# Leaving SyncE out of a skipped fallback: a two-way switch on four engines in place of an If on all five, with the fallback's DMAs issued by GpSimd

## Chip, cores, metric

One core of a Trainium2 chip. The metric is the device time of an execution in microseconds (us), given as the median of several executions. A profile is one such execution; its "span", the time from its first to its last instruction, is shorter than its measured time by 1.8 us here (before: 780.63 against 778.8).

## The reference

```python
def reference(A_x, A_wq, A_wk, A_wv, A_wo, B_x, B_w_gate, B_w_up, B_w_down):
    # A: attention, H = 32 query heads of 16, one shared key/value head; x is 1 x 2048 x 512, bf16
    #    q = x@wq; k = x@wk; v = x@wv; p = softmax(q k^T * 16**-0.5); o = p v; return o @ wo
    # B: (silu(x @ w_gate) * (x @ w_up)) @ w_down, with 1792 hidden columns
    x = A_x
    xn = _layernorm(x, axis=-1)
    s = _A_ref(xn, A_wq, A_wk, A_wv, A_wo)
    g = _silu(_B_ref(xn, B_w_gate, B_w_up, B_w_down))
    return x + s * g
```

## The kernel before

The kernel computes the softmax without subtracting row maxima. At the end it checks whether every denominator lies between 16 and 1e30. If one doesn't, a flag is set and a long exact path computes everything anew. With the inputs the flag is 0 and the exact path is jumped over. What matters here is the end of the program: the flag, the last four row blocks, their stores, and the conditional.

```python
    # flag: 1 if any of the 128 partition minima says "out of range"
    tadd("DVE", e_out_mul(LN, obk[0], dsts[0]))
    tadd("DVE", nc.vector.tensor_single_scalar(out=flag_i[:], in_=tq01[0:1, 0:1], scalar=P - 0.5, op=ALU.is_lt))
    loads, vals = nc.values_load_multi_w_load_instructions(flag_i[0:1, 0:1])   # all five engines
    flag = vals[0]
    tadd("SP", [l for l in loads if l.ins.engine == nc.sync.engine])
    fin_add(0, nc.gpsimd, "POOL")
    tadd("DVE", e_out_mul(LN + 1, obk[1], dsts[1]))
    tadd("DVE", e_out_mul(LN + 2, obk[2], dsts[2]))
    fin_add(2, nc.gpsimd, "POOL")
    tadd("DVE", [l for l in loads if l.ins.engine == nc.vector.engine])
    fin_add(1, nc.vector, "DVE")
    tadd("DVE", e_out_mul(LN + 3, obk[3], dsts[3]))
    fin_add(3, nc.vector, "DVE")
    for k in range(4):
        tadd("SP", e_out_st(LN + k))          # the last four stores, 128 KB each, on SyncE's queue
    MAIN.close()

    with tc.If(flag > 0):
        _exact_max_path(...)                  # long; its DMAs are nc.sync.dma_start
```

`tadd` fixes the order on an engine. In `_exact_max_path` three lines start DMAs (cut):

```python
                        nc.sync.dma_start(out=MR[row:row + 1, :], in_=tms[r0:r0 + NT, :])
    # ...
            nc.sync.dma_start(out=xr[:], in_=x_v[:, n, :])
    # ...
            nc.sync.dma_start(out=out_v[:, n, :], in_=res[:])
```

## Time and profile before

| | before |
|---|---|
| time, median of 3 | 781.96 us (780.98 to 782.83) |
| span of the profiled execution | 778.8 us |
| flag made, start | 769.94 us |
| VectorE's last add ends | 773.44 us |
| last store: issued, landed | 773.81, 776.07 us |
| SyncE's gap after its branch | 774.2 to 776.9 us |
| from the flag to the end of the span | 8.9 us |

"Landed" is the time of the last of a store's 16 semaphore updates; each is taken to stand for the part that one of the 16 DMA engines moves (the trace doesn't name the engine).

### The profile page before, as it was taken

The page shows a single profiled execution, that of the slowest core. Times are in us where ns is not written, and L with a number is a line of the kernel's source. Part 1 is how long each engine was busy: PE and PEld are TensorE (multiplying, and loading weights), DVE is VectorE, ACT ScalarE, POOL GpSimd, SP SyncE. Part 2 cuts the span into 40 slices and gives each one's busy share as a digit, 9 for nine tenths or more (in the row PEclk, how much of TensorE's full clock was granted, in tenths as well). Part 3 has the DMA queues.
Part 4 walks back from the last instruction along what each step waited for, and adds up shares of the span by engine and source line. Part 5 has one row for each costly group of instructions (what it writes and reads, how often), then busy time and mean ns, then how long its engine had stood idle before and what let it go on. Part 6 is the DMA issues. An engine that isn't in the chain of part 4 may idle for free.

```text
span 778.8 us, 20698 instructions
## 1 busy us (share of the span) xinstructions
PE 748.9 (96%) x9093; PEld 229.7 (29%) x9095; DVE 734.0 (94%) x920; ACT 756.9 (97%) x866; POOL 54.2 (7%) x59
## 2 busy tenths in 40 slices
PE   8999999999999999999999999999999999999995
PEld 3323223322222333322233322322223233322221
DVE  7689999999999999999999999999999999999995
ACT  6999999999999999999999999999999999999993
POOL 2100000000012000000001110000000300000101
PEclk9999999999999999999999999999999999999998
DMA  9400000000001000000000100000000000000001
GB/s 327 141 9 9 16 2 24 3 8 17 4 28 50 23 2 6 18 2 24 2 10 22 49 24 2 24 1 9 16 2 24 28 23 2 2 23 3 22 2 32
DMA packets 21193, 20.15 MB, mean 26 GB/s; under 512 B 8744, under 2 KB 17192, under 8 KB 21096
## 3 DMA queue, kind: packets, MB, share of 16 engines
q1 hardware_dynamic: 19512, 18.20, 7.7%
q8 instruction: 73, 1.20, 0.6%
q10 hardware_dynamic: 1584, 0.56, 0.3%
q14 instruction: 24, 0.20, 0.1%
HBM read 14.19 MB, written 2.34 MB: 21 GB/s over the span
## 4 chain that ended last, share of the span: by engine, by line
PE 48%; ACT 45%; DVE 5%; issue 1%; SPq 0%; DMA 0%; ACTq 0%; POOL 0%; DVEq 0%; POOLq 0%
ACT Pb L937 41%; PE ring L877 17%; PE m_ps L488 16%; PE o_ps L747 13%; ACT th L657 3%; DVE Bf L997 1%; ACT g_sb L937 1%; PE ring L433 1%; DVE Bf L1016 1%; ACT th L674 1%; DVE x_sb L997 0%; DVE Bf L1023 0%; PE ring L488 0%; DVE x_sb L1016 0%; PE ring L452 0%
## 5 line engine op out<-in xcount | busy, mean ns | idle before, releaser
L937 ACT ACTIVATE Pb<-ring 128x1024 bf16<-128x1024 f32 x772 | 730.7, 1202 | 2.1 <-PE ring L877 2.1
L877 PE MATMUL ring<-QB,KT 32*128 32x512 bf16 x2048 | 306.0, 382 | 15.6 <-ACT Pb L937 9.3
L997 DVE TENSOR_SCALAR Bf<-ring 128x1024 uint16<-128x1024 f32 x172 | 209.2, 1216 | 5.2 <-PE ring L877 3.7
L877 PEld LDWEIGHTS <-KT 32*128 32x128 bf16 x2048 | 94.1, 90 | 313.9 <-issue 307.4
L747 PE MATMUL o_ps<-Pb,VA 128*32 128x512 bf16 x1544 | 146.9, 385 | 0.0
L997 DVE TENSOR_SCALAR x_sb<-ring 128x1024 uint16<-128x1024 f32 x72 | 87.6, 1217 | 2.7 <-PE ring L877 2.4
L1016 DVE TENSOR_TENSOR Bf<-Bf,Bf 128x2048 f16<-128x2048 f16 x74 | 90.0, 1216 | 0.1
L747 PE MATMUL o_ps<-xnT,zw 128*32 128x512 bf16 x1092 | 83.1, 381 | 0.0
L488 PE MATMUL m_ps<-xnT,wu_sb 128*32 128x512 bf16 x896 | 72.6, 384 | 1.1 <-DVE ab L659 1.1
L488 PE MATMUL m_ps<-wd_sb,hT 128*32 128x512 bf16 x896 | 71.5, 383 | 0.1
L488 PE MATMUL m_ps<-xnT,wg_sb 128*32 128x512 bf16 x896 | 70.4, 384 | 0.0
L747 PE MATMUL o_ps<-Bf,VD 128*32 128x512 f16 x688 | 67.1, 385 | 0.4 <-DVE Bf L1016 0.3
L732 POOL TENSOR_TENSOR oT<-oa,rb 128x512 bf16<-128x512 f32 x15 | 22.7, 1514 | 614.2 <-DMA rb<-dscr 515.7
L1023 DVE TENSOR_SCALAR Bf<-Bf 128x2048 uint16<-128x2048 uint16 x86 | 60.4, 702 | 0.6
L747 PEld LDWEIGHTS <-VA 128*32 128x32 bf16 x1560 | 38.0, 94 | 53.8 <-issue 51.5
L1011 DVE TENSOR_SCALAR Bf<-Bf 128x2048 uint16<-128x2048 uint16 x74 | 52.1, 712 | 0.0
L657 ACT ACTIVATE th<-m_ps 128x512 f32<-128x512 f32 x56 | 43.7, 781 | 0.0
L659 DVE SCALAR_TENSOR_TENSOR ab<-th,m_ps 128x512 f32<-128x512 f32 x56 | 38.1, 680 | 4.2 <-ACT th L657 3.9
L663 DVE TENSOR_TENSOR hT<-ab,m_ps 128x512 bf16<-128x512 f32 x56 | 38.1, 680 | 2.1 <-PE m_ps L488 1.7
L747 PEld LDWEIGHTS <-VD 128*32 128x32 f16 x976 | 26.6, 94 | 38.9 <-issue 35.3
L747 PEld LDWEIGHTS <-zw 128*32 128x32 bf16 x1092 | 25.8, 95 | 25.5 <-issue 12.9
L1016 DVE TENSOR_TENSOR x_sb<-x_sb 128x2048 f16<-128x2048 f16 x24 | 29.2, 1215 | 0.0
(121 smaller groups left out, 414.3 us busy)
## 6 DMA issues: line engine op xcount, KB each, us to landing
rb<-dscr SPq DMA_DIRECT2D x15, 256.0 KB
out_dram<-xn SPq DMA_DIRECT2D x16, 128.0 KB, 1.9
dn<-oa SPq DMA_DIRECT2D x120, 2.0 KB, 1.7
oa<-oa SPq DMA_DIRECT2D x60, 32.0 KB, 2.0
wg_sb<-in_B_w_gate_dram SPq DMA_DIRECT2D x1, 1792.0 KB, 12.3
wu_sb<-in_B_w_up_dram SPq DMA_DIRECT2D x1, 1792.0 KB
wd_sb<-in_B_w_down_dram SPq DMA_DIRECT2D x1, 1792.0 KB, 19.7
x_sb<-in_A_x_dram SPq DMA_DIRECT2D x3, 512.0 KB
```

Of the source, the lines that this page charges most:

```text
L488: return [nc.tensor.matmul(out=dst[GRP * j:GRP * j + GRP, :], lhsT=w[:, GRP * j:GRP * j + GRP], rhs=rhs, start=start, stop=stop, tile_posi ...
L657: t_ = OP("ACT", 0.477, [a], lambda: nc.scalar.activation(out=th[i][:], in_=m_ps[:], func=ACT.Tanh, scale=0.5), (0,), name="tanh")
L659: s_ = OP("DVE", 0.6, [t_, ab_rel[i]], lambda: nc.vector.scalar_tensor_tensor(out=ab[i][:], in0=th[i][:], scalar=1.0, in1=m_ps[:], op0=ALU ...
L663: h = OP("DVE", 0.6, [b], lambda: nc.vector.tensor_tensor(out=hT[:, f, :], in0=ab[i][:], in1=m_ps[:], op=ALU.mult), (1,), name="hmul")
L732: return [pk, q], lambda eng: eng.tensor_tensor(out=oT[qs % 2][:, jj, :], in0=o0[:], in1=rbt[:], op=ALU.mult)
L747: r.append(nc.tensor.matmul(out=o_ps[GRP * g:GRP * g + GRP, :], lhsT=lhs, rhs=rhs, start=(n == 0), stop=(n == pv_total[(b, g)] - 1), tile_ ...
L877: return lambda: [nc.tensor.matmul(out=ring[sl][:, u * 512:(u + 1) * 512], lhsT=KT[half][GRP * g:GRP * g + GRP, t * P:(t + 1) * P], rhs=QB ...
L937: bi = nc.scalar.activation(out=buf, in_=ring[i][:], func=ACT.Exp, scale=escale, bias=ebias)
L997: lambda: nc.vector.tensor_scalar(out=U[:, hs], in0=ring[si][:], scalar1=ubias, scalar2=UINF, op0=ALU.add, op1=ALU.min), (1.5, u), name="p ...
L1011: o1 = OP("DVE", 0.6, [pa, pa0] + wrel, lambda: nc.vector.tensor_scalar(out=Bf[wi], in0=U, scalar1=0x3FF, scalar2=0x3800, op0=ALU.bitwise_and,
L1016: return lambda: eng.tensor_tensor(out=Bf[wi][:, a:z].bitcast(FP16), in0=Bf[wi][:, a:z].bitcast(FP16), in1=U[:, a:z].bitcast(FP16), op=ALU ...
L1023: o2 = OP("DVE", 0.6, o3, lambda: nc.vector.tensor_scalar(out=U, in0=U, scalar1=0x7C00, scalar2=None, op0=ALU.bitwise_and), (2, u, 1), nam ...
```

## The change

The intent is to take SyncE out of the conditional. SyncE issues the last stores, so it comes to the branch last, and its long jump ends the program. As SyncE must then issue nothing within the fallback, the fallback's DMAs go to GpSimd, and the If becomes a two-way switch on the four other engines, whose arm 0 is empty.

```diff
@@ three lines of _exact_max_path @@
-                        nc.sync.dma_start(out=MR[row:row + 1, :], in_=tms[r0:r0 + NT, :])
+                        nc.gpsimd.dma_start(out=MR[row:row + 1, :], in_=tms[r0:r0 + NT, :])
-            nc.sync.dma_start(out=xr[:], in_=x_v[:, n, :])
+            nc.gpsimd.dma_start(out=xr[:], in_=x_v[:, n, :])
-            nc.sync.dma_start(out=out_v[:, n, :], in_=res[:])
+            nc.gpsimd.dma_start(out=out_v[:, n, :], in_=res[:])
@@ the flag @@
-    loads, vals = nc.values_load_multi_w_load_instructions(flag_i[0:1, 0:1])
-    flag = vals[0]
-    tadd("SP", [l for l in loads if l.ins.engine == nc.sync.engine])
+    arm_engines = [mybir.EngineType.PE, mybir.EngineType.Activation, mybir.EngineType.DVE, mybir.EngineType.Pool]
+    loads, vals = nc.values_load_multi_w_load_instructions(flag_i[0:1, 0:1], engines=arm_engines, min_val=0, max_val=1,
+                                                           skip_runtime_bounds_check_because="is_lt writes 0 or 1")
@@ the conditional @@
-    with tc.If(flag > 0):
+    for arm in tc.Switch({e: vals[0] for e in arm_engines}, 2):
+        if arm == 0:
+            continue
         _exact_max_path(tc, nc, wo_sb, x_v, out_v, wq_sb, xnT, KT, VA, g2_sb, ident_bf, ident_f, qscale,
```

## The prediction

> **What bounds the kernel now.** I read the page first, for what limits the body, then what stands at the end of the span, because the diff touches nothing before it. The page's busy times and slices:
>
> ```profile
> span 778.8 us, 20698 instructions
> ...
> PE 748.9 (96%) x9093; PEld 229.7 (29%) x9095; DVE 734.0 (94%) x920; ACT 756.9 (97%) x866; POOL 54.2 (7%) x59
> ```
>
> ScalarE, TensorE and VectorE are all within a few per cent of the span, and the exponentials on ScalarE (772 of 1202 ns) carry it. None of this is in the fallback: the three engines run the main path and the fallback is jumped over, as the instruction count shows. So 770 us of the span are out of the change's reach and only the end is left.
>
> The chain of waits of the last stretch, in order of time, comes next:
>
> ```profile
> 769.94 0.13 DVE flag_i L1360
> 770.07 0.57 DVE ab L690
> ...
> 771.87 0.61 DVE oa L690
> 772.48 0.02 issue
> 772.50 0.93 DVE xn L695
> ```
>
> It stops at 773.43 although the span ends at 778.8: the last 5.4 us hold no compute, only sequencers. The window sums say the same (columns: stretch, its length, then busy us and count of PE, PEld, DVE, ACT, POOL, the clock, DMA share, GB/s):
>
> ```profile
> 774.20:776.90 2.70, 0.00 (x0) 0.00 (x0) 0.00 (x0) 0.00 (x0) 0.00 (x0) 0.50 0.35 110
> 776.90:778.80 1.90, 0.00 (x0) 0.00 (x0) 0.00 (x0) 0.00 (x0) 0.00 (x0) 0.50 0.01 4
> ```
>
> The timeline of SyncE and the listing of the If's own line (duration min/median/max in ns, then first and last start) give what fills them:
>
> ```profile
> 771.35 2.83 SPq L698 DMA_DIRECT2D out_dram<-xn  x4
> ```
>
> ```profile
> L1376 SPq EVENT_SEMAPHORE  x8: 17/17/17, 776.9 to 777.4; - x8
> L1376 ACTq COMPARE_BRANCH  x1: 50/50/50, 770.6 to 770.6; - x1
> L1376 PEldq COMPARE_BRANCH  x1: 3635/3635/3635, 770.7 to 770.7; - x1
> L1376 POOLq COMPARE_BRANCH  x1: 45/45/45, 771.9 to 771.9; - x1
> L1376 DVEq COMPARE_BRANCH  x1: 72/72/72, 772.5 to 772.5; - x1
> L1376 ACTq EVENT_SEMAPHORE  x1: 17/17/17, 773.5 to 773.5; - x1
> L1376 SPq COMPARE_BRANCH  x1: 45/45/45, 774.2 to 774.2; - x1
> ...
> L1376 DVEq EVENT_SEMAPHORE  x1: 21/21/21, 775.4 to 775.4; - x1
> ```
>
> And SyncE's own waits:
>
> ```profile
> SPq L1376 <- SPq L1376: 2.6, 1, 2.6
> ```
>
> The reader is to see that after its branch at 774.2 SyncE does nothing for 2.6 us, and that nobody else is named as having released it. VectorE is silent equally long after its branch (772.6 to 775.4, 2.8 us), ScalarE too (770.7 to 773.5, 2.8 us), TensorE for 3.6 us inside the branch. GpSimd, whose body of the If is empty, goes on after 0.1 us. So these are gaps of a jump over a large body, not waits for data. For four engines the gap lies beside other work. Only for SyncE, the last to branch since it branches behind the last store, is it on the path that sets the end.
>
> **What the Trainium skill says.** "Runtime: NRT & Kernel Launch", section "Instruction fetch mechanics": prefetch is sequential, and a taken branch to a target outside the window that is loaded stalls for a fetch. The trace agrees: 2.6 to 3.6 us where a body is jumped, 0.1 us where there is none. The page names no figure for the stall. "Advanced Engine Details and Errata", section "Control Flow Timing", gives compare-and-branch some 108 ns; the trace has 45 to 72 ns for the instruction itself, so the instruction isn't the cost. "DMA: Bandwidth & Descriptors", section "Anatomy of one DMA — SWDGE (gpsimd) path", has about 2.0 us fixed for a DMA, mostly the receipt of the write; the four last stores of this trace took 2.4 to 2.7 us from issue to landing, median 2.5, so the trace's figure is used.
>
> **The change part by part.** The order of the built programs shows the main path the same instruction for instruction, apart from the flag's handling. So the first 770 us: 0.
>
> (a) SyncE loses its load of the flag (0.48 us at 770.10). It stood before the first store, but that store is issued at 771.35 as GpSimd's add of 1.15 us from 770.17 ends at 771.32. Worth 0.
>
> (b) SyncE loses its branch, and with it the 2.6 us gap and the eight semaphore steps behind it, spaced 0.07 us (776.9 to 777.4). It now runs straight from the last store into the final waits. What ends these is the landing of the last store: issued at 773.81 (771.35 + 2.83 - 0.37), landing 2.3 to 2.4 us later, so at 776.1 to 776.2. In the kernel before this landing was hidden under the gap; now it takes the gap's place. The final list of waits has twelve entries instead of eight (four more steps, for the software-queue semaphores of GpSimd), but these stand first and are passed while the landing is awaited. Behind the last store's semaphore stand six more at 0.06 us, 0.4 us. Then comes the closing barrier: from SyncE's last such wait (777.9) to the end (778.8), 0.9 us. New end: 776.1 + 0.4 + 0.9 = 777.4. Gain 778.8 - 777.4 = 1.4 us.
>
> (c) The other four replace one compare-and-branch by a register set-up, a multiply-add, an indirect branch into a short arm 0, and at its end an unconditional branch over the fallback, with a prefetch hint at the arm's start. I take an estimate of 0.3 us for the additional steps (about five at 0.05 to 0.07 us, the spacing just read). The jump of 2.8 us stays. VectorE is the latest: 772.5 + 0.3, then its count step that waits for its own last add (773.4), then 2.8 us: 776.2 if the hint gains nothing, 775.6 if it starts the fetch at once. Both are before the 776.5 at which SyncE clears its list, but not by much. TensorE: 770.6 + 0.5 + 3.6 = 774.7. GpSimd, which skipped nothing before, now has the long body: flag loaded at 771.8, 0.5 us of set-up and arm, 2.8 us: 775.1. Off the path.
>
> (d) Arm 0 on GpSimd has to bring the eight semaphores of its software queues up to the count that arm 1 would leave. It does this at about 772.5, and SyncE waits for that; a like instruction takes 27 ns at the start of this trace. Off the path.
>
> (e) The 100 or so DMAs moved to GpSimd are in arm 1, which doesn't run: 0.
>
> Sum: 0 + 1.4 + 0 = 1.4 us of 782, 0.2%.
>
> **The rivals.** First, the full gap goes: 2.6 + 0.5 = 3.1 us, some 779 us. Against it stands the landing: 2.4 us after the last issue is not gone, and nothing in the change shortens it.
>
> Second, the jump turns up on another engine. If the indirect branch into arm 0 stalls too, VectorE pays twice: 772.8 + 2.8 + 0.1 + 2.8 = 778.5, against the 778.0 at which SyncE joins the barrier now; the end would be 779.3 and the time 0.5 us longer, 782.5. For it speaks that four engines show the stall at any long jump; against it that arm 0 is the next code in order and that GpSimd's short step took 0.1 us. I give it one in five. A milder form, in which the hint's fetch queues behind another, puts VectorE near 776.7 and the gain at 1.2.
>
> Third, the stores themselves shift. The second store's issue took 1.31 us (the listing of the store line has median 361 ns, maximum 1314), and this held back the third and fourth. If it is issued in 0.4, the last store leaves when VectorE's add ends at 773.43, and the landing comes 0.3 to 0.4 us earlier: gain 1.8. It falls together with a 16 KB instruction transfer in the same window (the queue of kind "instruction" moved two there), so with more such fetches from the new branches it could as well be longer, and a further 1 us would eat most of the gain.
>
> Fourth, a use of the software queue costs something outside the span at launch. The measured time exceeds the span by about 3 us already; the queue is declared in both programs, so I expect nothing.
>
> **Range and chances.** 781.96 - 1.4 = 780.6 us. The effect itself lies between -3 and +0.5; the three runs of before spread over 1.85 us, so a median of three is good to about 0.6. Together: 779.2 to 782.0 in 8 of 10. A change of 2% would need 15.6 us, three times all that happens after the last compute; so 0.98 for within 2%, 0.01 for either side, kept for something at launch that no view shows.
>
> **What would show it.** Right: SyncE has no instruction of the If's line and no flag load; its waits name the landing of the last store instead of itself, ending near 776.1; the distance from the last store's issue to the end of the span falls from 5.0 to about 3.6 us; GpSimd and VectorE show the long gap after their new branches but reach the barrier before SyncE. Wrong in step (b): the end is not tied to the landing. Wrong in step (c): VectorE's or GpSimd's last step comes behind SyncE's, with two gaps of 2.8 us. The prediction as a whole would be wrong if the body before 769 us changed its length, for which I see no reason.

## The result, and the profile after

| | before | after |
|---|---|---|
| time, median of 4 and range | 782.24 us (780.98 to 782.83) | 782.7 us (781.48 to 783.38) |
| span of the profiled execution | 778.8 us | 781.4 us |
| flag made, start | 769.94 us | 770.12 us |
| last store: issued, landed | 773.81, 776.07 us | 775.10, 780.08 us |
| from the flag to the end | 8.9 us | 11.3 us |

All outputs are right. The ratio after to before is 1.0006, with a 95% interval of 0.9988 to 1.0025. A ratio is the mean time of one kernel's runs over that of the other's of the same rounds, so it is not quite the ratio of the medians. The kernels take the same time, as the most likely of the three classes said; but 782.7 us lies 0.7 above the predicted range, and the gain of 1.4 us isn't there.

First, whether the body moved. The page of after, then its chain of waits at the end (start, duration in us, what):

```profile
span 781.4 us, 20718 instructions
...
PE 747.5 (96%) x9093; PEld 229.2 (29%) x9095; DVE 734.1 (94%) x920; ACT 757.0 (97%) x866; POOL 54.0 (7%) x59
```

```profile
770.13 0.13 DVE flag_i L1360
...
772.69 0.93 DVE xn L695
```

The work is the same, and the compute ends at 773.62 instead of 773.44. The difference of 2.6 us between the two spans therefore arises almost wholly after the last compute. SyncE's own waits (engine, line, what it waited for: us in total, times, longest), then the timeline of SyncE:

```profile
SPq L1406 <- DMA out_dram<-xn: 2.3, 2, 2.1
SPq L1406 <- PEq L1406: 0.7, 2, 0.5
```

```profile
771.53 5.43 SPq L698 DMA_DIRECT2D out_dram<-xn  x4
```

SyncE's wait for itself is gone, and a wait for the landing of the stores stands in its place. That much is as predicted. SyncE isn't quite without a branch under the switch, though:

```profile
L1406 SPq COMPARE_BRANCH  x1: 43/43/43, 777.0 to 777.0; - x1
```

Its next instruction comes 0.4 us later, which the wait for the landing covers here.

But issuing the four stores took 5.43 us, against 2.83 before. The listing of the store's line has the reason. Its columns are the duration of one issue in ns (min/median/max), then first and last start; the line below gives the landings that the view could pair (the first and the third store). Before:

```profile
L698 SPq DMA_DIRECT2D out_dram<-xn x4: 349/378/1314, 771.3 to 773.8; - x4
...
DMA to landing us min/median/max: 2.4/2.5/2.7
```

After:

```profile
L698 SPq DMA_DIRECT2D out_dram<-xn x4: 343/1101/1882, 771.5 to 775.1; - x4
...
DMA to landing us min/median/max: 4.6/4.7/4.8
```

Before, one of four issues was long (1314 ns); after, two were (1882 and 1859 ns), and the landings, counted from the start of the issue, took about twice as long. The last store's landing was 2.7 us longer than before: 1.5 us of this is its longer issue, and nearly all of the rest comes from one late part. Of the 16 parts of after's last store, 15 had landed at 778.32 and the last at 780.08; of its first store, 14 at 773.25 and the last two at 775.51 and 776.09. So behind the issue one or two parts were late, not the store as a whole. What else ran on the DMA engines in these microseconds is in the DMA view for 771 to 775 us (queue, kind: packets, MB, share of the 16 engines' time). Before:

```profile
q14 instruction: 3, 0.02, 2.6%
q8 instruction: 1, 0.02, 1.8%
```

After:

```profile
q14 instruction: 6, 0.05, 9.4%
q8 instruction: 2, 0.03, 6.6%
```

These are fetches of instructions: four before, eight after, and together 16.0% of the DMA engines' time instead of 4.4%. Each is one packet: 16 KB on q8, 8 KB on q14. Over the whole tail there are 8 before and 13 after. q8 is taken to be TensorE's: it has 74 fetches in a span, TensorE some 18,200 matmuls and weight loads, and a hint on TensorE alone later started one there. That leaves q14 to the other engines.

Last, the new branches. The listing of the conditional's line in after:

```profile
L1406 PEldq COMPARE_BRANCH  x2: 358/2678/4998, 771.2 to 771.9; - x2
L1406 DVEq COMPARE_BRANCH  x2: 60/68/75, 772.9 to 773.8; - x2
...
L1406 DVEq DRAIN  x1: 70/70/70, 778.2 to 778.2; - x1
```

There are two branches for each engine: into arm 0, and from there over the fallback. TensorE's second branch took 5.0 us (before 3.6), and VectorE was silent from 773.8 to 778.2, 4.4 us (before 2.8). Both were ready before SyncE, whose last store landed at 780.08.

Three theories were set against each other from here. **Theory 1**: the instruction fetches of the far branches share the DMA engines with the last four stores, hold up their issues and landings, and so eat what SyncE's branch had cost. **Theory 2**: GpSimd's software-queue DMAs, and the semaphores that an engine must bring up for them in arm 0, cost the time. **Theory 3**: there is nothing there but the spread from run to run, or a fixed tail.

### The profile page after: what moved, and what is told of

Read it like the earlier page. It is cut to its first block, busy times and chain, and to the rows that moved or that the text cites. A ratio compares the mean times of both kernels' runs of the same rounds, so it can differ in the third digit from the quotient of the medians.

```text
span 781.4 us, 20718 instructions
## 1 busy us (share of the span) xinstructions
PE 747.5 (96%) x9093; PEld 229.2 (29%) x9095; DVE 734.1 (94%) x920; ACT 757.0 (97%) x866; POOL 54.0 (7%) x59
## 4 chain that ended last, share of the span: by engine, by line
PE 47%; ACT 44%; DVE 6%; issue 1%; POOL 0%; SPq 0%; DMA 0%; ACTq 0%; DVEq 0%; POOLq 0%
ACT Pb L937 39%; PE ring L877 17%; PE m_ps L488 16%; PE o_ps L747 13%; ACT th L657 3%; DVE Bf L997 1%; ACT g_sb L937 1%; DVE Bf L1016 1%; ACT th L674 1%; DVE x_sb L997 0%; DVE Bf L1023 0%; PE ring L488 0%; DVE hT L663 0%; DVE Bf L1011 0%; DVE x_sb L1011 0%
```

## The experiments

In the tables, "store issues" are the durations of the four issues in ns, "landing" is from issue to the last part's landing for the last store, and "fetches" are instruction fetches in the tail. Kernels of one group were run on the same chip and share its runs of the kernel before.

### First group: the If without SyncE, no conditional, hints, and a repeat

**if_four**: the change without the switch. SyncE is out and GpSimd issues, but the plain If stays.

```diff
 # against before: the three DMAs on nc.gpsimd and the flag loaded by four engines, as in the change
-    tadd("SP", [l for l in loads if l.ins.engine == nc.sync.engine])
     with tc.If(flag > 0):      # kept
```

> The changed kernel with the plain If in place of the Switch: SyncE takes no part, the fallback's DMAs are GpSimd's, the software-queue semaphores are there. 'Tail' is from the start of the flag's instruction on VectorE to the end of the span: 8.9 us before, 11.3 after, in the profiled runs. Theory 1 (fetch traffic: the Switch makes each of four engines fetch one more block of instructions, and these transfers hold up the last stores on the DMA engines they share): the tail is 7.0 to 7.8 us, the last store lands within 2.7 us of its issue, issues take 0.4 us but for one or two of 1.3; time 0.1 to 0.25% below before. Theory 2 (the software queue of GpSimd or its semaphores cost it): tail about 11 us as in after, stores late. Theory 3 (nothing but spread from run to run; stores are held up at random): tail anywhere from 7 to 11, time equal to after.

**no_cond**: the changed kernel with the flag still computed, but with neither the loads nor the fallback (a floor, not a kernel to use).

```diff
-    loads, vals = nc.values_load_multi_w_load_instructions(...)
-    tadd("DVE", [l for l in loads if l.ins.engine == nc.vector.engine])
-    for arm in tc.Switch({e: vals[0] for e in arm_engines}, 2):
-        ...
```

> No flag, no conditional, no fallback: the floor (right for these inputs, which never take the fallback). All theories: no engine jumps far. Theory 1: next to no instruction transfers after 770 us, four issues of 0.35 to 0.4 us, the last store lands 2.0 to 2.4 us after its issue, tail 6.3 to 6.9 us counted from the time at which the flag would be made (VectorE's first product of the last group, 0.6 us earlier, is the mark); time 0.2 to 0.35% below before. Theory 3: some stores would still be issued in over 1 us or land over 4 us late.

**if_hint**: if_four with a branch prefetch hint on each of the four engines, moved ahead of the branch.

```diff
+    tc.mark_branch_hint_location("fallback", "LikelyTaken", engines=[PE, Activation, DVE, Pool])
-    with tc.If(flag > 0):
+    with tc.If(flag > 0, label="fallback"):
+    # after the build: each hint to the 63rd (PE), 6th (ACT), 22nd (DVE), 5th (POOL)
+    # instruction from the end of its engine's main block
```

> if_four, with a prefetch hint for the If's branch on each of the four engines some microseconds ahead of it, before the last stores. Theory 1: the transfers of the targets move ahead of the stores, the gap after the branches goes from 2.8 us to under 0.5, and only the sequential fetches behind the targets are left among the stores: tail 6.5 to 7.5 us, the time equal to if_four or up to 0.1% lower. Theory 2 or 3: no better than if_four. If a hint isn't held until its branch or blocks the sequential prefetch, the gap stays or an engine stalls before the branch, and the time is that of if_four or up to 3 us longer.

**after_again**: the changed kernel once more.

> The changed kernel once more. Theory 1: tail 10 to 12 us again, with two or more of the four stores issued in over 1 us and the last landing over 3.5 us after its issue; time within 0.15% of before, on the slow side. Theory 3: the tail differs by 2 us or more from the first profiled run.

| | time (n = 5) | ratio to before (95%) | store issues, ns | landing, us | fetches | flag to end, us |
|---|---|---|---|---|---|---|
| before (n = 9) | 781.64 (780.42 to 782.29) | 1 | | | | |
| if_four | 781.56 (780.05 to 781.96) | 0.9998 (0.9985 to 1.0012) | 344, 1601, 745, 353 | 3.2 | 8 | 9.0 |
| no_cond | 778.64 (778.44 to 779.26) | 0.9963 (0.9949 to 0.9976) | 344, 344, 332, 332 | 1.7 | 1, after the stores | 6.7 |
| if_hint | 779.32 (778.99 to 779.47) | 0.9971 (0.9957 to 0.9984) | 343, 375, 1514, 450 | 1.8 | 7, and 1 ahead | 7.8 |
| after_again | 781.68 (780.48 to 782.99) | 1.0001 (0.9987 to 1.0015) | 344, 343, 1203, 2461 | 5.5 | 13 | 11.1 |

The stores of no_cond, in the listing of their line:

```profile
L698 SPq DMA_DIRECT2D out_dram<-xn x4: 332/338/344, 771.9 to 774.0; - x4
...
DMA to landing us min/median/max: 1.7/1.7/1.7
```

This is the store undisturbed: 0.34 us to issue, 1.7 us to land (2.0 to 2.4 had been expected). Theory 3 had expected issues of over 1 us or landings of over 4 us here too, and there is none. "The" landing, 2.3 to 2.5 us, was already a disturbed one. The trace of before had the floor all along, in the listing of the same line over all of its 16 stores:

```profile
L698 SPq DMA_DIRECT2D out_dram<-xn x16: 332/361/1314, 232.2 to 773.8; - x16
...
DMA to landing us min/median/max: 1.7/1.9/2.7
```

no_cond also bounds the whole question: the conditional costs 3.0 us (781.64 - 778.64). And its times lie within 0.8 us, where before's lie within 1.9: part of the spread from run to run leaves with the conditional.

if_four answers whether leaving SyncE out is worth 1.4 us by itself. SyncE's waits there:

```profile
SPq L1405 <- DMA out_dram<-xn: 2.2, 2, 1.7
```

Its gap is gone and a landing stands in its place, as in after, and the time is before's within 0.1 us. The interval reaches down to 0.9985, or 1.2 us, so a small gain isn't excluded by this group, but 1.4 is. The lost gain therefore doesn't need the switch to explain it. This was also a miss for Theory 1 as it had been put: it had laid the loss to the switch's additional fetches and expected a tail of 7.0 to 7.8 us and a time 0.1 to 0.25% below before. The If's own eight fetches are enough (tail 9.0 us, landing 3.2 us).

after_again repeats the trace of after: 13 fetches, two long issues, a late landing. Yet its median is if_four's within 0.1 us, although the traces differ by 2 us in the tail. The profiled execution of after_again took 782.73 us, its second slowest of five; if_four's took 780.97, its second fastest. So the medians don't separate switch from If, and a trace is one draw out of a spread.

if_hint gained 0.29%, more than expected (at most 0.1% below if_four). TensorE's hint started its fetch early (a 16 KB fetch at 769.08, 4.3 us before VectorE's last add ends), and its branch over the fallback shrank from 3.9 us in if_four to 0.9 us. The hints on ScalarE and VectorE started none: the gaps behind their branches remained (ScalarE 770.6 to 773.2, VectorE 772.5 to 775.9). These two hints had run at 762.2 and 760.6, and GpSimd's at 689.3: a place counted in instructions says little about the time.

### Second group: repeat of before, a later switch, no software-queue DMAs, no hints

**before_again**: the kernel before once more.

> The kernel before, profiled once more. In six traces the flag is made at 769.8 to 770.5 us, so the body is the same and only the tail differs; yet the median times of before and after are equal, though the profiled tails were 8.9 and 11.1 to 11.3. Theory 1 (instruction transfers of the branching engines hold up the last stores, in before too, and by an amount that varies from run to run): the first profiled run of before was a lucky one; a second has a tail of 9.0 to 10.8 us, with the last store landing over 2.6 us after its issue, later than SyncE's own gap ends. Theory 3 (a fixed tail of 8.9 in before, and something outside the span that favours after): tail 8.7 to 9.0 again and the time still that of after.

**switch_late**: the changed kernel with the flag made behind VectorE's last add, so that the engines branch when the stores are nearly out.

```diff
-    tadd("DVE", nc.vector.tensor_single_scalar(out=flag_i[:], ...))
-    arm_engines = ...; loads, vals = ...
-    tadd("DVE", [l for l in loads if l.ins.engine == nc.vector.engine])
     fin_add(3, nc.vector, "DVE")
+    tadd("DVE", nc.vector.tensor_single_scalar(out=flag_i[:], ...))
+    arm_engines = ...; loads, vals = ...
+    tadd("DVE", [l for l in loads if l.ins.engine == nc.vector.engine])
```

> The changed kernel with the flag made and loaded after VectorE's last add instead of 3.5 us before it, so that the engines branch once the stores are nearly all issued. Theory 1: the stores are back to issues of 0.33 to 0.45 us and landings 1.7 to 2.2 us after them; the end is set by the branching engines instead, some 6.0 to 7.0 us after the last add (after: 7.6 to 7.8), so the time is no longer, perhaps 0.05 to 0.15% shorter, although the branch comes over 3 us later. Theory 2 (software queue) or a cost of the Switch itself: stores as slow as in after, and the time 1 to 3 us longer.

**switch_nodma**: the changed kernel with no DMA at all in the fallback, so that GpSimd has no software-queue semaphores to bring up. The fallback would be wrong if it ran; it never runs with these inputs.

```diff
+        nc.vector.memset(MR[:], 0.0)
-                        nc.gpsimd.dma_start(out=MR[row:row + 1, :], in_=tms[r0:r0 + NT, :])
+                        pass
-            nc.gpsimd.dma_start(out=xr[:], in_=x_v[:, n, :])
+            nc.vector.memset(xr[:], 0.0)
-            nc.gpsimd.dma_start(out=out_v[:, n, :], in_=res[:])
```

> The changed kernel with a fallback that issues no DMA at all (it would give a wrong result if it were taken, which these inputs never do): no software queue, no semaphores of it, GpSimd's arms all but empty. Theory 1: the tail stays at 10 to 11.5 us, stores issued in over 1 us and landing over 3.5 us after, 12 to 13 instruction transfers in the tail; time equal to after within 0.1%. Theory 2 (the software queue or its semaphores): tail 7 to 9 us and the time 0.2 to 0.4% below after.

**switch_nohint**: the changed kernel without the prefetch hints that the switch puts at the head of its arms.

```diff
+    for b in nc.m.functions[0].blocks:
+        b.instructions = [i for i in b.instructions if i.opcode != "BranchPrefetchHint"]
```

> The changed kernel without the prefetch hints at the head of the Switch's arms. Theory 1 in the form that each engine fetches three blocks (the one behind arm 0, the target of the long jump, the one behind that): the count of transfers stays at 12 to 13, tail 10 to 11.5 us, time within 0.1% of after. If it is the hint that crowds the transfers (two of an engine at once), they spread out: stores issued faster, tail 9 to 10, and the time about 0.1% lower.

| | time (n = 4) | ratio to before (95%) | store issues, ns | landing, us | fetches | flag to end, us |
|---|---|---|---|---|---|---|
| before (n = 7) | 781.28 (780.19 to 781.82) | 1 | | | | |
| before_again | 781.18 (780.57 to 781.61) | 1.0001 (0.9985 to 1.0018) | 348, 1313, 383, 443 | 3.5 | 8 | 9.3 |
| switch_late | 783.55 (783.01 to 784.13) | 1.0030 (1.0013 to 1.0047) | 343, 346, 332, 332 | 1.7 | 13, all after the last issue | 8.5 (flag made at 773.4, not about 770) |
| switch_nodma | 781.63 (780.88 to 782.68) | 1.0005 (0.9988 to 1.0022) | 344, 347, 1174, 2412 | 4.9 | 13 | 10.4 |
| switch_nohint | 783.23 (782.98 to 783.66) | 1.0029 (1.0012 to 1.0045) | 344, 344, 1200, 2253 | 5.2 | 14 | 10.8 |

before_again shows that before's stores are disturbed too: its last store landed at 777.01, 0.3 us after the end of SyncE's gap at 776.74. In the kernel before, the gap merely covers most of these landings.

switch_late is the cleanest test of Theory 1's mechanism. It has the same 13 fetches as after; only their time differs (the first at 774.96, when all stores are issued). The listing of its store line and of TensorE's branches:

```profile
L698 SPq DMA_DIRECT2D out_dram<-xn x4: 332/338/346, 771.4 to 773.5; - x4
...
DMA to landing us min/median/max: 1.7/1.7/1.7
```

```profile
L1406 PEldq COMPARE_BRANCH  x2: 353/2620/4888, 774.6 to 775.3; - x2
```

The stores are back at the floor of no_cond, to 0.02 us. Moved apart, fetches and stores do not hurt each other; together they do. (The jumps moved along with their fetches, so switch_late alone can't tell the two apart. TensorE's hint helps here: it leaves the branches of the other engines where they were and brings only TensorE's fetches forward.) The time was nevertheless expected to fall and rose by 0.3%, and the end came 8.4 us after the last add instead of 6.0 to 7.0: now four engines jump at once, up to 3.5 us later than in after (ScalarE's first branch at 774.5 for 771.0), five of the fetches take 2.0 to 2.9 us each where 0.3 to 1.7 us is usual with an If, TensorE's branch ends at 780.2, and the last engines reach the end at 780.9. So the jumps cannot be put off for nothing.

switch_nodma fells Theory 2: without a software-queue DMA and without the semaphores, the two long issues, the late landing and the time are those of the changed kernel. In after the instruction in question is short, and it is done 8 us before the end:

```profile
L1376 POOLq INC_SWDGE_SEM  x1: 177/177/177, 773.1 to 773.1; - x1
```

switch_nohint held in its trace (the stores and the number of fetches are the switch's, but for one more fetch at the very end) and missed in its time: 783.23 us against 781.63 for switch_nodma on the same chip. The hints of the arms are thus worth about 1.6 us here, with switch_nodma standing for the changed kernel, which didn't run in this group. The record has the spans of all four executions of each: their medians are 781.0 and 779.8, so 1.2 us lie within the span, and 0.4 to 0.7 in the time outside it (2.2 to 2.5 us in place of 1.8). The profiled spans alone, 780.8 and 780.4, show only 0.4 of the first. Where the time within the span goes is not explained, nor is the time outside it (no_cond too has 2.1 us there).

### Third group: TensorE's fetch alone taken out of the way

TensorE's target is the one fetch that a hint was seen to move. Two kernels with that hint, one with SyncE in the If and one without, ask whether leaving SyncE out gains the predicted 1.4 us once less stands in the stores' way.

**before_hint_pe**: the kernel before with TensorE's hint alone.

```diff
+    tc.mark_branch_hint_location("fallback", "LikelyTaken", engines=[mybir.EngineType.PE])
-    with tc.If(flag > 0):
+    with tc.If(flag > 0, label="fallback"):
+    # after the build: the hint to the 63rd instruction from the end of TensorE's main block
```

> The kernel before (SyncE takes part in the If, the DMAs are its own) with a prefetch hint for TensorE's branch alone, about 5 us ahead of it. It shows what SyncE's gap is worth once the stores are less disturbed. Theory 1: TensorE's target (16 KB) comes before the stores; SyncE's gap of 2.6 us after the last store stays and sets the end: tail 8.6 to 9.2 us, the time 0.1 to 0.2% below before and 0.1 to 0.2% above the same hint with SyncE left out. If SyncE's gap is worth nothing even then: equal to that kernel.

**if_hint_pe**: if_four with the same three edits.

> The If on four engines without SyncE and the same hint on TensorE alone. The hints on ScalarE and VectorE in the earlier run started no transfer, so this should equal that run: tail 7.3 to 8.3 us, the end set by the landing of the last store or by VectorE's own jump, the time 0.25 to 0.32% below before. Against the kernel with SyncE in and the same hint it gains the 0.8 to 1.5 us that the prediction had promised for leaving SyncE out.

**if_hint_near**: if_hint with ScalarE's and VectorE's hints nearer to their branches (4th and 12th instruction from the end) and none on GpSimd.

```diff
-        ahead = {PE: 63, Activation: 6, DVE: 22, Pool: 5}
+        ahead = {PE: 63, Activation: 4, DVE: 12}
```

> The same, with hints on ScalarE and VectorE too, but 3 to 4 us ahead of their branches instead of 8 to 12. If they take now, the gaps behind these two branches fall from 2.6 to 3.4 us to under 0.6, and their targets come before the first store: tail 6.7 to 7.5 us, time 0.3 to 0.38% below before. If not: equal to the hint on TensorE alone.

**if_four_again**: if_four once more, in this group.

> The If on four engines without SyncE and without a hint, again, beside the three others on one chip. Theory 1: its time scatters over 1.5 us or more, with a median within 0.1% of before; tail 8 to 10.5 us with the last landing over 2.7 us after its issue. If leaving SyncE out were worth its 1.4 us by itself, it would be 0.18% below before.

| | time | ratio to before (95%) | store issues, ns | landing, us | fetches | flag to end, us |
|---|---|---|---|---|---|---|
| before (n = 11) | 781.77 (780.30 to 782.77) | 1 | | | | |
| before_hint_pe (n = 5) | 780.33 (780.19 to 781.54) | 0.9987 (0.9974 to 1.0000) | 348, 1471, 383, 955 | 2.4 | 7, and 1 ahead | 9.5 |
| if_hint_pe (n = 6) | 779.05 (778.71 to 779.62) | 0.9970 (0.9958 to 0.9982) | 344, 1532, 698, 353 | 1.7 | 7, and 1 ahead | 7.4 |
| if_hint_near (n = 5) | 779.27 (778.81 to 779.87) | 0.9972 (0.9958 to 0.9985) | 344, 1801, 714, 353 | 1.8 | 7, and 1 ahead | 7.7 |
| if_four_again (n = 6) | 781.01 (779.12 to 781.65) | 0.9989 (0.9974 to 1.0005) | 343, 1286, 383, 1064 | 3.9 | 8 | 9.0 |

SyncE's waits in before_hint_pe, then in if_hint_pe:

```profile
SPq L1377 <- SPq L1377: 2.5, 1, 2.5
```

```profile
SPq L1406 <- DMA out_dram<-xn: 0.6, 2, 0.3
```

and TensorE's branch in if_hint_pe:

```profile
L1378 PEldq COMPARE_BRANCH  x1: 499/499/499, 770.5 to 770.5; - x1
```

With the hint, SyncE's own gap of 2.5 us still ends the program of before_hint_pe. Take SyncE out, and 0.6 us of waiting for a landing is left: 780.33 - 779.05 = 1.28 us gained, and the ranges of the two don't touch (780.19 to 781.54 and 778.71 to 779.62). The tails of the two profiled runs, 9.5 and 7.4 us, differ by more, but the profiled run of before_hint_pe was the slowest of its five; its tail also missed the 8.6 to 9.2 us expected. The gain of 1.28 us is nearly the 1.4 us of the prediction, and it appears where the landing of the last store is back at 1.7 us. Without the hint, the same step gave 0.08 us (if_four) and 0.76 us (if_four_again), neither apart from zero by its interval; the second interval still admits 1.4.

if_hint_near did no more than if_hint_pe: gaps of 2.5 to 3.1 us remain on ScalarE and VectorE, and no fetch started early but TensorE's. The trace has ScalarE's hint 6.5 us and VectorE's 4.4 us ahead of their branches (8.3 and 11.8 us in if_hint), not the 3 to 4 us that had been aimed at, so a hint still nearer is untested, and why these start nothing stays open. TensorE's own hint, executed at 765.4 in if_hint_pe, started its fetch only at 768.04.

if_hint_pe is the best usable version, not to be told apart from if_hint and if_hint_near by its time: 0.30% faster than before, and 0.3% below the changed kernel too by their ratios to before (0.9970 against 1.0001 and 1.0006). It keeps the SyncE-free conditional, drops the switch, and adds one hint. It is short of 2%, as anything in this tail must be.

## Why the prediction was right or wrong

**How it read the profile: right in its outline.** The body didn't move, all of the effect lies after the last compute, SyncE's gap vanishes, and the landing of the last store takes its place. One reading is wrong: "the four last stores of this trace took 2.4 to 2.7 us" gives the two stores that the view could pair. By their semaphore updates the four took 2.7, 3.2, 2.4 and 2.3 us.

**Step (a), the flag load of SyncE, 0: right.** The first store is issued at 771.53, 0.03 us after GpSimd's add ends, as before.

**Step (b), gain 1.4 us: this is the step that failed, in one term of its sum.** The sum was landing + 0.4 + 0.9 us. The two small terms are exact: after's span is 780.08 + 1.3 = 781.4. The same sum gives 777.2 for if_hint_pe (775.90 + 1.3) and 779.1 for if_four (777.84 + 1.3), both the measured spans. What failed is "the landing comes 2.3 to 2.4 us later, so at 776.1 to 776.2". It took one disturbed draw of the profile before as a constant of the hardware, and let the program change everything around it without changing it. The draw was a lucky one besides: 27 executions of before have a median span of 779.7 us (778.3 to 780.9), and the profiled one had 778.8. In before_again the prediction's own sum gives 777.01 + 1.3 = 778.3 against a span of 778.9: 0.6 us, with nothing changed but the draw. In after, the issue came 1.29 us later (775.10 for 773.81) and the landing took 2.72 us longer (4.98 for 2.26): together 4.0 us against a term that should have stayed. Undisturbed it is 1.7 us (no_cond, switch_late), so it can even fall below the prediction's figure. Where it did (if_hint_pe), the step's gain came out at 1.28 us.

**Step (c), the other four engines off the path: right in its conclusion, wrong in its sizes.** VectorE was expected to be ready at 775.6 to 776.2 and was at 778.2, GpSimd at 775.1 and was at 777.9; TensorE's jump was taken as 3.6 us and was 5.0. Only because the stores were late as well did this remain off the path: against the expected SyncE it would have set the end. Had the estimate asked how many fetches the switch adds (13 for 8), it could have met the same cause from this side.

**Steps (d) and (e), GpSimd's semaphores and the moved DMAs, 0: right**, by switch_nodma; the instruction took 177 ns where 27 ns were estimated, off the path.

**The rivals.** The first, that the full gap goes, fell: even with the stores least disturbed, SyncE's leaving gained 1.28 us. The third had the direction and the cause: "with more fetches from the new branches it could as well be longer, and a further 1 us would eat most of the gain". It was placed as a footnote to one issue of 1.31 us; in fact two issues and all landings were affected, and the last landing came 4 us later. The second rival put VectorE's end at 778.5, near the 778.2 seen, but by luck: it reckoned with two gaps of 2.8 us, where there was one of 0.5 and one of 4.4. The fourth fell: the time outside the span is 1.8 us in both kernels. The "3 us" of the prediction came from setting the median of one set of runs against the span of another, faster execution (780.63 us).

**The range.** It allowed the effect to reach +0.5 us, which on top of 781.96 is 782.5, and before's median to be off by 0.6, but was centred on the gain, so that 782.0 was its upper end. The effect measured is 0.0 us (after_again: 781.68 for 781.64) to +0.5 us (782.7 for 782.24), neither apart from zero by its interval. The range's own text had named this as possible; the weight on it was too small. Before's own median also rose, from 781.96 to 782.24, with a fourth run.

**What is shown and what is not.** Shown: with fetches beside them the stores are slow (12 traces), and without (no_cond) or with the same number later (switch_late) they are at the floor; the software queue isn't the cause; SyncE's leaving gains 1.28 us when TensorE's target is fetched ahead. Argued only: which single fetch held up which store, as the trace names no DMA engine for a packet. But the coincidences in time are regular. Under the If, the long issue of the second store ends 0.33 to 0.43 us after the end of a 16 KB fetch in all seven traces that have one; under the switch, that of the fourth store ends 0.40 us after an 8 KB fetch in all four traces with disturbed stores. Where one part of the last store came over 0.5 us behind the other 15 (seven traces), it landed 1.08 to 1.20 us after a 16 KB fetch ended; the last store of before, with a part 0.4 us behind, doesn't fit this. In if_hint, if_hint_pe and if_hint_near, where no such fetch falls behind the last issue, all 16 parts landed within 0.2 us. And in all 56 stores the eighth part landed 1.25 to 1.33 us after the end of the issue: a disturbance lengthens the issue or delays a few parts, and leaves the rest alone. Open: why ScalarE's and VectorE's hints start no fetch; why the profiled runs of after and after_again fall near the slow end of their spread while the switch's median equals that of the If, so that by time alone the switch's 13 fetches cannot be told from the If's 8; what the slower executions of before wait for, as none was profiled; and why removing the switch's hints costs 1.6 us.

## What to carry to other kernels

A skipped branch over a long body is paid twice: by the engine that jumps, and by whatever transfer runs beside the fetches. So when a wait at the end of a program is removed, ask not only which wait is next, but whether its duration was measured under the conditions of the new program; a landing time from one trace is a sample, and its floor (here 1.7 us) and its disturbed size (here up to 5.5 us) should both be known. Before an engine is taken out of a conditional, take the fetches out of the way of the last stores, here by one hint for TensorE ahead of its branch: that, not the switch, let the removal gain its microsecond.

## What the Trainium skill lacked or had wrong

- "Runtime: NRT & Kernel Launch", section "Instruction fetch mechanics". It gives no figure for the stall of a taken branch: the traces have 2.5 to 3.4 us on ScalarE, VectorE and SyncE with an If, 3.6 to 3.9 us on TensorE without a hint, and under the switch 4.1 to 5.7 us on ScalarE, VectorE and GpSimd and 4.5 to 5.0 us on TensorE. It speaks of refills in 16 KiB blocks: here the fetches on one queue are 16 KB, those on the other 8 KB. It calls the cost of crossing a block "mostly hidden" and has no figure for what fetches cost a kernel's own transfers: with fetches in the same microseconds, issues of stores rose from 0.34 to as much as 2.46 us and landings from 1.7 to as much as 5.5 us. It has about 200 ns per register for a register load: the load of the one-element flag, from an on-chip tile, took 0.46 to 0.63 us in these traces.
- "Advanced Engine Details and Errata", section "Control Flow Timing". It has about 108 ns for a compare-and-branch: the recorded instruction takes 38 to 90 ns on all engines but TensorE, and what follows it is 0.1 us (GpSimd with an empty body) to 5.7 us.
- "DMA: Bandwidth & Descriptors", section "Anatomy of one DMA — SWDGE (gpsimd) path". It has about 2.0 us fixed, for the other path: on SyncE's queue a store of 128 KB landed 1.7 us after the start of its issue where nothing disturbed it, its transfer included.
- No page covers branch prefetch hints. TensorE's hint started its fetch 2.6 to 3.7 us later and cut its branch from 3.6 us or more to 0.5 us (0.9 us in if_hint); ScalarE's and VectorE's hints ahead of an If started none; without the switch's own hints the time was about 1.6 us longer.
